# An adaLN, H3 and SwiGLU kernel on one core: the front of the program in another order, with both half loads of modulation rows ahead of the third chunk's return

## The chip, the core and the metric

The kernel runs on one core of a Trainium2 chip. The metric is the device time of one execution in microseconds, and every figure below is for that one core. A difference of 0.2% is about 1.2 us here.

## What is computed

The sequence has S = 2048 positions and D = 512 channels, the feed-forward layer F = 1792 columns. Everything is float32.

```python
mod = (silu(c) @ w_mod).reshape(1, 6, 1, 512)      # six modulation rows
sa, ca, ga, sb, cb, gb = mod[:, 0], ..., mod[:, 5]
h = layernorm(x) * (1 + ca) + sa
# H3 mixer with q = h
k_shift = causal_conv4(k, shift_k)                 # four taps for each channel
kv = k_shift * v
y = irfft(rfft(kv, 2 * S) * rfft(ssm_k, 2 * S))[:S] + kv * ssm_D
x = x + ga * (h * y)
h = layernorm(x) * (1 + cb) + sb
x = x + gb * ((silu(h @ w_gate) * (h @ w_up)) @ w_down)
```

## The kernel before

The channels are worked in four chunks of 128. For each chunk c the program builds `kv` on VectorE (`tap`, `times_v`), turns it and takes the first stage of its Fourier transform on TensorE (`x_turn`, `x_first`), does the same for the long filter (`k_first`, `k_turn`), and swaps 32x32 blocks on VectorE (`swap_x`). The second stage, the product with the filter and the first inverse stage go by halves of a chunk, numbered n = 2c and 2c + 1: `x3` and `x_sum` make three inputs, `product3` multiplies them with three filter products, `inv3` goes back. For chunks 0, 1 and 2 the result X must be turned through memory: `put(c)` writes 2 MB to DRAM, and `get(c)` fetches it back with rows and positions exchanged, in four DMAs of 512 KB. For chunk 3 that turn is done by VectorE straight out of PSUM (`inv3s`). "The third chunk's return" in the title is `get(2)`.

`y_pe(t, *cs)` takes the last inverse stage for position tile t (512 positions) and chunks cs; it needs the matrix `ei` (`load_einv`) and the returned chunks. VectorE gates the result and adds it to x (`y_gate` with `add_y`, or `y_into` in one, which also collects the statistics of the second layernorm). The first layernorm's gate is made ahead of that by `gate_n` (ScalarE) and `gate_p` (GpSimd or VectorE). The modulation rows come in three parts `wm` of 2 MB, loaded in halves; for the third part `mod_row(2, h)` does a half's products on TensorE, `mod_out` copies the row out, `mod_T` turns it into columns.

The second layernorm of tile t ends in `rs1` (VectorE), `rs2` and `rs3` (GpSimd), four `norm1` (ScalarE). Then four `norm_t` transpose on TensorE, `norm_s` scales, and `hi1` and `lo1` split each operand into a high part and a low rest. `gu_pe` is the first gate and up product of the feed-forward layer. `warm(n)` issues n matmuls whose result nobody reads. The feed-forward loop that follows (seven products in place of eight, weights split and kept) is the longest part of the kernel.

What stands where is written out by hand: between the lines 1204 and 1595 some 390 calls stand in a list, and every engine works through its own instructions in the order of that list, since each helper issues with `keep_in_program_order`. All loads and stores are issued by SyncE on one queue, in the order of the list as well. Eight DMA semaphores go round, so a DMA is issued only when the one eight places before it has landed. Buffers come from tagged pools, and the strings in `SLOTS` say which buffer each new tile takes; `ps` gives the four pairs of PSUM banks. A tile that takes a buffer waits for the last reader of the tile before it. The third part of the modulation rows shares its buffer with the first-stage filter of chunk 3, so its load waits for the last `k_turn(3, ...)`:

```python
def mod_load(p_, h=None):
    if p_ not in WM:
        WM[p_] = (f16 if p_ == 2 else b16)("wm", (P, 8, D))
    for k in (0, 1) if h is None else (h,):
        t = slice(4 * k, 4 * k + 4)
        sp.dma_start(WM[p_][:, t], wmod[p_][:, t])
```

Every instruction is recorded at line 40, the helper that keeps the order, so the profile is read by the names of the tiles: `iv` is `inv3`, `pk` is `product3`, `px` is `x3`, `kt` is `k_turn`, `s` on TensorE a first stage, `y` is `y_pe`, `mr` is `mod_row`, `pm` is `mod_T`, `nt` is `norm_t`, `g` is `gu_pe`, `away` the DRAM copy of a chunk, `wm` a part of the modulation rows, `ei` the matrix of the last inverse stage, `ss` the long filter, `rsb` the second layernorm's scale. A `dn` is a down product; `a`, `b` and `c` are products of the feed-forward loop.

Of the kernel before, what the change touches and what calls it, by code (L numbers as in the profile page):

```python
# [43 lines left out]
def adaln_h3_swiglu(ctx, tc, q, k0, v0, kT, vT, ssm, dskip, wgu, wdn, wmod, e_fwd, e_inv, w_c, out):  # L44
# [9 lines left out]
        "e8": "301245670142561074612740340143104134104134104134150364051304650314056304",  # L54
        "b16": "0112345024024453024",
        "k2": "012021021020121020121020121020121020121020121012021012021012021012021012021012021012",
        "ps": "012301230123012031203120312031203120312013201320132013210321032103103210321032103210321032102310231023102310321032103210321213120023012120310",
        "r4": "01234012430012342013424301430123403402143201342014320134201432013420143240310234213014324031",
        "one": "456723017425036241736412506425173421750621507341573062570634170346250362417364125064251730256731546317027513643105725601341076526370140753623157047561321065745630120376546713025",
# [299 lines left out]
    def swap_x(n):  # L359
        swap(X[n // 4], n % 4)  # L360
# [842 lines left out]

    load_k0(0)
    diag(0, e=act)
    diag(2, e=dve)
    load_k0(1)
    warm(16)
    small_in(e=act)
    p_tap0(e=dve)  # L1210
    p_tap(1, 0, e=dve)
    p_tap(2, 0, e=dve)
    load_v0(0)
    load_k(1)
# [24 lines left out]
    load_ssm(0, 1)
    load_ssm(0, 2)  # L1240
    load_ssm(0, 3)
    load_v(1)
    room()
    tap(1, 1)
    tap(1, 2)
    skip(0, e=dve)
    load_k(2)
    tap(1, 3)
    times_v(1, 3, e=pool)
    load_v(2)  # L1250
    swap_x(2)
    swap_x(3)
    k_first(0, 2, e=act)
    k_first(0, 1, e=act)
    times_v(1, 2, e=pool)
    k_first(0, 3, e=act)
    times_v(1, 1, e=pool)
    k_first(0, 0, e=act)
    tap0(2, e=act)
    warm(5)  # L1260
    k_turn(0, 0, e=act)
    k_turn(0, 1, e=dve)
    tap(2, 1)
    times_v(1, 0, e=pool)
    k_turn(0, 2, e=act)
    x_turn(1, 1, e=act)
    k_turn(0, 3, e=act)
    tap(2, 2)
    load_ssm(1)
    x_turn(1, 0, e=act)  # L1270
    k_first(1, 3, e=act)
    skip(1, e=pool)
    k_first(1, 0, e=act)
    x_first(1, 0, e=act)
    k_first(1, 1, e=act)
    k_first(1, 2, e=act)
    mod_rep(e=dve)
    x_first(1, 1, e=act)
    load_wc()
    load_k(3)  # L1280
    k_turn(1, 0, e=act)
    k_turn(1, 3, e=act)
    tap(2, 3)
    times_v(2, 0, e=pool)
    times_v(2, 1, e=pool)
    tap0(3, e=dve)
# [12 lines left out]
    tms(3, 2, e=act)
    tap(3, 1)  # L1300
    x_sum(0, e=pool)
    tma(3, 2, 3, e=pool)
    swap_x(4)
    x_turn(2, 1, e=act)
    tma(3, 2, 1, e=pool)
    tma(3, 2, 2, e=pool)
    swap_x(6)
    tms(3, 3, e=act)
    tma(3, 3, 3, e=pool)
    product3(1, 1)  # L1310
    tma(3, 3, 1, e=pool)
    mod_load(0)
    tma(3, 2, 0, e=pool)
    tma(3, 3, 0, e=pool)
    product3(0, 0)
    load_ssm(3)
    mod_mul(0, 0, e=act)
    load_ssm(2)
    product3(1, 2)
    product3(0, 1)  # L1320
    product3(0, 2)
    product3(1, 0)
    k_turn(1, 2, e=act)
    x_first(2, 1, e=act)
    swap_x(7)
    swap_x(5)
    load_v(3)
    mod_load(1)
    swap_x(8)
    mod_part(0, 0, e=pool)  # L1330
    load_x(0)
    tma(3, 3, 2, e=pool)
    load_einv()
    times_v(3, 1, e=pool)
    skip(2, e=dve)
    mod_mul(0, 1, e=act)
    times_v(3, 2, e=pool)
    inv3(1, e=act)
    inv3(0, e=act)
    put(0)  # L1340
    load_x(2)
    load_x(3)
    times_v(3, 3, e=pool)
    k_turn(1, 1, e=act)
    swap_x(10)
    x3(3, 2, e=dve)
    x3(2, 1, e=act)
    x3(3, 1, e=act)
    swap_x(9)
    skip(3, e=dve)  # L1350
    times_v(3, 0, e=pool)
    k_first(2, 0, e=act)
    k_first(2, 2, e=act)
    x_sum(3, e=dve)
    get(0)
    x3(2, 2, e=act)
    x_sum(2, e=pool)
    mod_mul(1, 0, e=act)
    mod_part(1, 0, e=pool)
    product3(3, 2)  # L1360
    product3(3, 0)
    product3(3, 1)
    mod_mul(1, 1, e=act)
    product3(2, 0)
    product3(2, 2)
    mod_part(1, 1, e=pool)
    mod_part(0, 1, e=pool)
    mod_part(0, 2, e=pool)
    do_stats(1, 0)
    mod_part(1, 2, e=pool)  # L1370
    product3(2, 1)
    k_first(2, 3, e=act)
    k_first(2, 1, e=act)
    x_turn(3, 0, e=act)
    inv3(3, e=act)
    inv3(2, e=act)
    do_stats(2, 0)
    k_turn(2, 0, e=act)
    x_turn(3, 1, e=act)
    k_turn(2, 1, e=act)  # L1380
    k_turn(2, 3, e=act)
    swap_x(11)
    put(1)
    get(1)
    x_first(3, 0, e=act)
    mod_part(0, 3, e=pool)
    mod_part(1, 3, e=pool)
    mod_bc(1)
    do_stats(0, 0)
    do_stats(0, 1)  # L1390
    do_stats(1, 1)
    x_first(3, 1, e=act)
    do_stats(2, 1)
    mod_bc(0)
    x3(5, 1, e=act)
    x3(5, 2, e=act)
    x3(4, 2, e=act)
    k_turn(2, 2, e=act)
    do_stats(3, 0)
    do_stats(3, 1)  # L1400
    x3(4, 1, e=act)
    x_sum(4, e=pool)
    swap_x(14)
    x_sum(5, e=pool)
    mod_mix()
    gate_n(2, 0, e=dve)
    k_first(3, 1, e=act)
    k_first(3, 0, e=act)
    k_first(3, 2, e=act)
    gate_n(0, 0, e=act)  # L1410
    gate_p(0, 0, 1, e=pool)
    load_w(1)
    k_first(3, 3, e=act)
    gate_n(3, 0, e=act)
    swap_x(15)
    swap_x(12)
    gate_n(0, 1, e=act)
    gate_p(0, 2, 1, e=pool)
    gate_n(1, 0, e=act)
    product3(4, 0)  # L1420
    product3(4, 2)
    gate_n(2, 1, e=act)
    product3(5, 0)
    product3(4, 1)
    product3(5, 1)
    product3(5, 2)
    swap_x(13)
    inv3(4, e=act)
    inv3(5, e=act)
    k_turn(3, 0, e=act)  # L1430
    k_turn(3, 2, e=act)
    gate_p(0, 3, 1, e=pool)
    put(2)
    k_turn(3, 1, e=act)
    gate_p(2, 0, 1, e=dve)
    gate_p(2, 2, 1, e=dve)
    x3(7, 1, e=act)
    x3(7, 2, e=act)
    gate_p(1, 0, 1, e=dve)
    mod_load(2, 0)  # L1440
    get(2)
    mod_load(2, 1)
    x_sum(7, e=pool)
    y_pe(0, 0, 1)
    gate_n(3, 1, e=act)
    gate_p(3, 0, 1, e=dve)
    gate_p(3, 2, 1, e=pool)
    k_turn(3, 3, e=act)
    gate_p(0, 1, 1, e=dve)
    x3(6, 1, e=act)  # L1450
    y_into(0, 0, 1)
    x3(6, 2, e=act)
    x_sum(6, e=pool)
    product3(7, 0)
    product3(7, 2)
    product3(7, 1)
    product3(6, 0)
    gate_n(1, 1, e=act)
    gate_p(1, 3, 1, e=pool)
    w8_hi(1)  # L1460
    product3(6, 1)
    gate_p(1, 1, 1, e=pool)
    product3(6, 2)
    inv3s(7)
    inv3s(6)
    y_pe(2, 0, 1)
    gate_p(2, 1, 1, e=pool)
    gate_p(2, 3, 1, e=pool)
    y_gate(2, 0, 1)
    y_pe(1, 0, 1)  # L1470
    gate_p(1, 2, 1, e=pool)
    mod_row(2, 0)
    load_w(0)
    y_pe(0, 3)
    gate_p(3, 1, 1, e=pool)
    y_into(0, 3)
    y_pe(0, 2)
    mod_row(2, 1)
    mod_out(2, e=act)
    w8_lo(1, e=pool)  # L1480
    y_into(0, 2)
    y_pe(2, 2, 3)
    rs1(0)
    mod_T()
    y_pe(1, 2, 3)
    rs2(0)
    rs3(0)
    y_pe(3, 0, 1)
    w8_hi(0)
    w8_lo(0, e=pool)  # L1490
    norm1(0, 0, e=act)
    norm1(0, 1, e=act)
    load_w(2)
    load_wd(0)
    wd_mul(0, e=pool)
    norm1(0, 2, e=act)
    norm1(0, 3, e=act)
    norm_t(0, 0)
    norm_s(0, 0, e=act)
    hi1("B11", 0, e=act)  # L1500
    y_gate(2, 2, 3)
    warm(5)
    norm_t(0, 1)
    norm_s(0, 1, e=act)
    acts_room()
    wd_hi(0)
    y_into(1, 0, 1)
    y_into(1, 2, 3)
    rs1(1)
    norm_t(0, 2)  # L1510
    norm_t(0, 3)
    norm_s(0, 2, e=act)
    hi1("B11", 1, e=act)
    lo1("B11", 1, e=dve)
    norm_s(0, 3, e=act)
    lo1("B11", 0, e=pool)
    hi1("B21", 0, e=act)
    gate_p(3, 3, 1, e=pool)
    y_gate(3, 0, 1)
    add_y(3, 0, 4, (0, 1), e=dve)  # L1520
    rs2(1)
    rs3(1)
    y_pe(3, 2, 3)
    lo1("B21", 0, e=pool)
    y_gate(3, 2, 3)
    norm1(1, 0, e=act)
    norm1(1, 1, e=act)
    gu_pe(0, 0, 0)
    hi1("B21", 1, e=act)
    lo1("B21", 1, e=dve)  # L1530
    add_y(3, 0, 4, (2, 3), e=dve)
    norm1(1, 2, e=act)
    room()
    gu_pe(1, 0, 0)
    gu_pe(1, 0, 1)
    gu_pe(0, 0, 1)
    load_w(3)
    norm1(1, 3, e=act)
    gu_pe(0, 0, 2)
    norm_t(1, 0)  # L1540
    norm_t(1, 1)
    add_y(2, 0, 4, (2, 3), e=dve)
    norm_s(1, 0, e=act)
    hi1("B12", 0, e=act)
    norm_t(1, 2)
    norm_t(1, 3)
    norm_s(1, 1, e=dve)
# [231 lines left out]
```

## Time and profile before

| | us |
|---|---|
| median of 3 runs | 581.48 |
| lowest and highest | 580.92 and 582.07 |
| the profiled execution, its own time | 579.46 |
| its span in the profile | 577.7 |
| TensorE busy in the span | 571.7 (99%) |
| VectorE busy in the span | 448.3 (78%) |
| ScalarE busy in the span | 306.4 (53%) |
| GpSimd busy in the span | 318.0 (55%) |
| first product of the feed-forward loop (`a`) starts | 182.11 |

A time of the profile counts from the start of the span. An engine's share over the whole span is a mean of two unlike stretches: the front up to about 182 us, where all five engines have much to do, and the loop behind it, where TensorE alone is full. The queue of SyncE, called SPq, issues the DMAs, and the time from issue to landing is the DMA's.

### The profile page before, as it was taken

The numbers are of one execution on the slowest core, as the hardware profiler recorded it, in microseconds if no ns is written. First come the engines' busy times: TensorE is split into PE (matmuls) and PEld (weight loads), VectorE is DVE, ScalarE is ACT, GpSimd is POOL, SyncE is SP. The second block draws the span as 40 slices with busy tenths as digits, with TensorE's granted clock in tenths as the row PEclk, the third lists the DMA queues.
The fourth block names the chain that finished last, engine by engine and source line by source line (L and its number), as shares of the span: only waits on it lengthen the run. The fifth ranks groups of instructions, "written<-read, shape, count | busy, mean of one in ns | idle before, by whom it ended". The sixth has DMA issues, their size and how long they took to land.

```text
span 577.7 us, 10729 instructions
## 1 busy us (share of the span) xinstructions
PE 571.7 (99%) x4262; PEld 462.5 (80%) x4262; DVE 448.3 (78%) x622; ACT 306.4 (53%) x471; POOL 318.0 (55%) x298
## 2 busy tenths in 40 slices
PE   9999999999999999999999999999999999999997
PEld 9985476546888888888887888888888888888886
DVE  4999999998998766666576579858686868686766
ACT  3999989951754544445454566343424343434330
POOL 1349897689737866757475676461606161515210
PEclk9999999999999999999999999999999999999999
DMA  8966998998215454284939970454343434343403
GB/s 315 411 256 261 379 251 227 235 235 205 69 37 200 148 216 165 40 281 145 283 140 257 250 319 1 149 190 171 117 160 124 160 123 161 127 162 127 163 1 145
DMA packets 54435, 106.98 MB, mean 185 GB/s; under 512 B 19441, under 2 KB 36209, under 8 KB 48370
## 3 DMA queue, kind: packets, MB, share of 16 engines
q1 hardware_dynamic: 54386, 106.31, 56.0%
q8 instruction: 33, 0.54, 0.4%
q14 instruction: 16, 0.13, 0.1%
HBM read 71.69 MB, written 34.60 MB: 184 GB/s over the span
## 4 chain that ended last, share of the span: by engine, by line
PE 86%; DVE 5%; DMA 4%; ACT 1%; SPq 1%; issue 1%; POOL 0%; ACTq 0%; POOLq 0%; DVEq 0%
PE a L40 22%; PE dn L40 14%; PE c L40 11%; PE b L40 6%; PE da L40 6%; PE s L40 4%; PE g L40 4%; PE dc L40 3%; PE iv L40 3%; PE pk L40 3%; DMA wm<-in_wmod 2%; PE kvt L40 2%; PE px L40 2%; DMA away<-X 1%; PE kt L40 1%; PE db L40 1%
## 5 line engine op out<-in xcount | busy, mean ns | idle before, releaser
L40 PE MATMUL a<-op,wsum 128*128 128x512 f32 x432 | 110.9, 392 | 0.3 <-ACT r L40 0.2
L40 PEld LDWEIGHTS a<-op,wsum 128*128 128x128 f32 x432 | 78.7, 188 | 15.7 <-ACT r L40 0.7
L40 PE MATMUL dn<-wd,acts 128*128 128x512 f32 x360 | 90.4, 389 | 0.0
L40 PEld LDWEIGHTS dn<-wd,acts 128*128 128x128 f32 x360 | 67.5, 188 | 14.0
L40 ACT COPY p<-a 128x512 f32<-128x512 f32 x50 | 29.3, 587 | 57.2 <-PE a L40 57.2
L40 POOL TENSOR_TENSOR wa<-ws,wa 128x512 fp32r<-128x512 f32 (+1 forms) x28 | 32.9, 1196 | 41.1 <-ACT wa L40 41.1
L40 DVE TENSOR_TENSOR x<-x,dn 128x512 f32<-128x512 f32 (+1 forms) x65 | 43.4, 672 | 12.8 <-PE dn L40 12.5
L40 POOL TENSOR_TENSOR tb<-wds 128x256 f32<-128x256 f32 x12 | 8.9, 740 | 64.1 <-DVE wds L40 64.1
L40 DVE TENSOR_TENSOR b<-r,c 128x512 f32<-128x512 f32 x24 | 16.7, 696 | 32.9 <-ACT sg L40 32.9
L40 ACT COPY r<-a 128x512 f32<-128x512 f32 x24 | 14.1, 586 | 50.7 <-PE a L40 50.7
L40 PE MATMUL c<-op,wa 128*128 128x512 f32 x156 | 40.0, 392 | 0.0
L40 PE MATMUL c<-op,wsum 128*128 128x512 f32 x156 | 39.6, 389 | 0.0
L40 DVE STREAM_TRANSPOSE X<-X 128x1024 f32<-128x1024 f32 x16 | 37.6, 2415 | 0.8 <-ACT X L40 0.8
L40 POOL TENSOR_TENSOR wsum<-sr,wsum 128x512 fp32r<-128x512 f32 x28 | 38.1, 1381 | 0.0
L40 PE MATMUL b<-op,wa 128*128 128x512 f32 x144 | 36.9, 391 | 0.0
L40 POOL TENSOR_TENSOR wd<-wds,wd 128x512 fp32r<-128x512 f32 x14 | 18.3, 1329 | 29.1 <-ACT wd L40 29.1
L40 PEld LDWEIGHTS c<-op,wsum 128*128 128x128 f32 x156 | 29.3, 188 | 6.1
L40 DVE TENSOR_TENSOR x<-x,da 128x512 f32<-128x512 f32 x48 | 32.7, 681 | 1.2 <-PE da L40 1.1
L40 PEld LDWEIGHTS c<-op,wa 128*128 128x128 f32 x156 | 28.5, 188 | 5.7 <-DVE b L40 0.4
L40 PEld LDWEIGHTS b<-op,wa 128*128 128x128 f32 x144 | 26.3, 188 | 4.9
L40 POOL TENSOR_TENSOR s<-s,bcs 128x512 f32<-128x512 f32 x22 | 28.0, 1287 | 0.9
L40 POOL TENSOR_TENSOR sr<-ws 128x256 f32<-128x256 f32 x28 | 24.8, 885 | 5.3 <-issue 4.4
(193 smaller groups left out, 1351.1 us busy)
## 6 DMA issues: line engine op xcount, KB each, us to landing
ds<-wsum SPq DMA_DIRECT2D x12, 1024.0 KB, 8.0
wsum<-ds SPq DMA_DIRECT2D x12, 1024.0 KB, 6.4
dw<-wa SPq DMA_DIRECT2D x12, 768.0 KB, 6.3
wa<-dw SPq DMA_DIRECT2D x12, 768.0 KB, 4.3
ws<-in_wgu SPq DMA_DIRECT2D x16, 512.0 KB, 5.4
wds<-in_wdn SPq DMA_DIRECT2D x14, 512.0 KB, 7.1
wm<-in_wmod SPq DMA_DIRECT2D x6, 1024.0 KB, 10.1
away<-X SPq DMA_DIRECT2D x3, 2048.0 KB, 11.8
```

The costliest lines, as they stand in the source:

```text
L40: return lambda *a, **k: self.tc.keep_in_program_order(f(*a, **k))
```

## The change

Only the list of calls and the `SLOTS` strings differ; every helper and the loop behind the front are the same text. Nearly every line of the list has another place. The sum of the work hardly changes: the same 26 `warm` matmuls in other places, the four `skip` instructions on one row of `ss` on GpSimd where three were on VectorE, and some elementwise steps on other engines. The places that the prediction speaks of, cut from the diff, with one of the `SLOTS` strings:

```diff
-        "b16": "0112345024024453024",
+        "b16": "0123450202530015430",
...
+    warm(5)
     load_k0(0)
...
+    skip(3, e=pool)
+    x_sum(3, e=pool)
...
-    warm(5)
...
-    load_einv()
...
-    skip(3, e=dve)
...
-    x_sum(3, e=dve)
...
+    load_einv()
...
+    warm(5)
...
+    put(2)
...
+    mod_load(2, 0)
+    mod_load(2, 1)
...
-    put(2)
...
-    mod_load(2, 0)
-    get(2)
-    mod_load(2, 1)
...
+    get(2)
...
+    mod_row(2, 0)
+    mod_row(2, 1)
+    y_pe(2, 0, 1)
...
+    mod_T()
...
     y_pe(0, 3)
...
     y_pe(0, 2)
-    mod_row(2, 1)
...
+    rs2(0)
...
-    mod_T()
...
-    warm(5)
...
+    add_y(2, 0, 4, (0, 1), e=pool)
```

On SyncE's queue the place is the return of the third chunk, with a `put` and a `get` of a chunk ahead of it (the numbers at the names tell tiles apart, and differ between the two programs). Before:

```order
L40 DMA away_1108<-X_400 128x4096
L40 DMA X_400<-away_1108 32x32x128 x4
L40 DMA ws<-in_wgu 128x1024
L40 DMA away_1498<-X_558 128x4096
L40 DMA wm<-in_wmod 128x2048
L40 DMA X_558<-away_1498 32x32x128 x4
L40 DMA wm<-in_wmod 128x2048
L40 DMA ws<-in_wgu 128x1024 x2
```

And in the change:

```order
L40 DMA away_1292<-X_413 128x4096
L40 DMA X_413<-away_1292 32x32x128 x4
L40 DMA ws<-in_wgu 128x1024
L40 DMA ei<-in_e_inv 128x2048
L40 DMA away_1482<-X_753 128x4096
L40 DMA wm<-in_wmod 128x2048 x2
L40 DMA X_753<-away_1482 32x32x128 x4
L40 DMA ws<-in_wgu 128x1024
```

The second half of the modulation rows has moved from behind the four DMAs of the return to ahead of them, and the load of `ei`, which stood far ahead of this place, now stands behind a load of weights (`ws`).

On TensorE the place is what follows the last inverse stage of chunk 3. Before, with X_195, X_400, X_558 and X_1114 for chunks 0 to 3:

```order
L40 MATMUL iv<-xs,wc 64x512 x48
L40 MATMUL y<-X_195,ei 64x128 x8
L40 MATMUL y<-X_400,ei 64x128 x8
L40 MATMUL y<-X_195,ei 64x128 x8
L40 MATMUL y<-X_400,ei 64x128 x8
L40 MATMUL mr<-wm,crep 32x512 x8
L40 MATMUL y<-X_1114,ei 64x128 x8
L40 MATMUL y<-X_558,ei 64x128 x8
L40 MATMUL mr<-wm,crep 32x512 x8
L40 MATMUL y<-X_558,ei 64x128 x8
L40 MATMUL y<-X_1114,ei 64x128 x8
L40 MATMUL pm<-thirty,mrow 128x1 x8
```

In the change, with X_203, X_413, X_753 and X_1118 for the same chunks:

```order
L40 MATMUL iv<-xs,wc 64x512 x48
L40 MATMUL mr<-wm,crep 32x512 x16
L40 MATMUL y<-X_203,ei 64x128 x8
L40 MATMUL y<-X_413,ei 64x128 x8
L40 MATMUL pm<-thirty,mrow 128x1 x8
L40 MATMUL y<-X_1118,ei 64x128 x8
L40 MATMUL y<-X_753,ei 64x128 x16
L40 MATMUL y<-X_1118,ei 64x128 x8
L40 MATMUL y<-X_753,ei 64x128 x8
L40 MATMUL y<-X_1118,ei 64x128 x8
L40 MATMUL y<-X_203,ei 64x128 x8
L40 MATMUL y<-X_413,ei 64x128 x8
```

Both halves of the modulation row and its turn `pm` now stand ahead of the first `y` that reads chunk 3 or chunk 2, and one pair of `y` that stood there has gone behind.

On GpSimd the place is the end of the second layernorm of tile 0 and what follows it. Before:

```order
L40 TENSOR_TENSOR s_1290<-s_1290,bcs 128x512 x2
L40 TENSOR_TENSOR wg<-ws,wg 128x512 x2
L40 TENSOR_TENSOR rsb_1864<-rsb_1864,mhalf 128x4
L40 TENSOR_TENSOR rsb_1864<-rsb_1864 128x4
L40 TENSOR_TENSOR wg<-ws,wg 128x512 x2
L40 TENSOR_TENSOR wds<-wds,bcs 128x1024
L40 TENSOR_TENSOR op<-hraw,op 128x512
L40 TENSOR_TENSOR s_1290<-s_1290,bcs 128x512 x2
```

In the change:

```order
L40 TENSOR_TENSOR s_1353<-s_1353,bcs 128x512 x2
L40 TENSOR_TENSOR rsb_1849<-rsb_1849,mhalf 128x4
L40 TENSOR_TENSOR rsb_1849<-rsb_1849 128x4
L40 TENSOR_TENSOR wg<-ws,wg 128x512 x2
L40 TENSOR_TENSOR wds<-wds,bcs 128x1024
L40 TENSOR_TENSOR op<-hraw,op 128x512
L40 TENSOR_TENSOR x_718<-x_718,s_1368 128x4x256
L40 TENSOR_TENSOR op<-hraw,op 128x512
```

An addition into x (`add_y`) now stands on GpSimd between the low rests of two operands of the first feed-forward product.

More of the change, by code (lines that the diff above doesn't have):

```diff
@@ L1314, in adaln_h3_swiglu @@
[L1314 to L1319, printed above, removed]
+    x3(0, 2, e=act)
+    tms(3, 2, e=dve)
+    x3(0, 1, e=act)
+    x_sum(0, e=pool)
+    times_v(2, 3, e=pool)
+    skip(2, e=pool)
+    product3(1, 0)
+    tms(3, 3, e=act)
+    mod_mul(1, 1, e=act)
+    mod_load(0)
+    product3(1, 1)
+    product3(1, 2)
+    times_v(2, 1, e=pool)
+    k_turn(1, 0, e=dve)
+    mod_mul(1, 0, e=act)
     product3(0, 1)
     product3(0, 2)
-    product3(1, 0)
@@ new lines, in adaln_h3_swiglu @@
+    x_first(2, 0, e=act)
+    x_first(2, 1, e=act)
+    swap_x(5)
+    k_first(2, 0, e=act)
+    k_first(2, 3, e=act)
+    x3(2, 1, e=act)
+    swap_x(7)
+    x3(2, 2, e=act)
+    x3(3, 1, e=act)
+    x3(3, 2, e=act)
+    k_first(2, 2, e=act)
+    do_stats(2, 0)
+    swap_x(10)
+    swap_x(11)
+    x_sum(2, e=pool)
+    product3(2, 1)
+    product3(2, 2)
+    mod_mul(0, 0, e=act)
+    k_first(2, 1, e=act)
+    mod_rep(e=act)
+    product3(2, 0)
+    skip(3, e=pool)
+    x_sum(3, e=pool)
+    mod_mul(0, 1, e=act)
@@ L1368, in adaln_h3_swiglu @@
+    product3(3, 2)
+    product3(3, 1)
+    product3(3, 0)
+    times_v(3, 1, e=pool)
+    inv3(2, e=act)
+    inv3(3, e=act)
+    x3(5, 1, e=act)
+    times_v(3, 0, e=pool)
+    x_turn(3, 0, e=act)
+    k_turn(2, 0, e=act)
+    k_turn(2, 2, e=act)
+    times_v(3, 3, e=pool)
+    times_v(3, 2, e=pool)
+    mod_part(0, 1, e=pool)
+    mod_part(0, 0, e=pool)
+    x_turn(3, 1, e=act)
+    k_turn(2, 3, e=act)
+    k_turn(2, 1, e=act)
+    load_x(3)
+    room()
     mod_part(0, 2, e=pool)
+    load_x(1)
@@ L1369, in adaln_h3_swiglu @@
+    mod_part(0, 3, e=pool)
+    x_first(3, 0, e=act)
     do_stats(1, 0)
[L1370 to L1386, printed above, removed]
+    x_first(3, 1, e=act)
+    mod_bc(0)
     mod_part(1, 3, e=pool)
-    mod_bc(1)
@@ new lines, in adaln_h3_swiglu @@
+    get(0)
+    k_first(3, 1, e=act)
+    swap_x(15)
+    put(1)
+    k_first(3, 0, e=act)
+    k_first(3, 3, e=act)
+    k_first(3, 2, e=act)
+    product3(5, 2)
+    mod_bc(1)
+    mod_mix()
+    product3(4, 0)
+    gate_n(1, 0, e=act)
+    gate_p(1, 0, 1, e=pool)
+    product3(4, 1)
+    gate_n(2, 0, e=act)
+    gate_n(0, 0, e=act)
+    get(1)
+    product3(5, 1)
+    product3(4, 2)
+    gate_n(3, 0, e=act)
+    gate_n(3, 1, e=act)
+    load_w(2)
+    load_einv()
+    gate_p(0, 0, 1, e=pool)
@@ L1519, in adaln_h3_swiglu @@
-    y_gate(3, 0, 1)
-    add_y(3, 0, 4, (0, 1), e=dve)
+    hi1("B21", 0, e=act)
+    room()
+    norm_s(0, 3, e=act)
+    add_y(2, 0, 4, (0, 1), e=pool)
+    y_pe(3, 0, 1)
+    gu_pe(1, 0, 0)
+    y_gate(3, 0, 1)
+    gu_pe(0, 0, 0)
+    norm_s(0, 1, e=act)
+    hi1("B11", 1, e=act)
+    lo1("B11", 1, e=pool)
+    gu_pe(0, 0, 1)
+    gu_pe(1, 0, 1)
     rs2(1)
     rs3(1)
-    y_pe(3, 2, 3)
-    lo1("B21", 0, e=pool)
-    y_gate(3, 2, 3)
     norm1(1, 0, e=act)
-    norm1(1, 1, e=act)
-    gu_pe(0, 0, 0)
@@ L1529, in adaln_h3_swiglu @@
-    hi1("B21", 1, e=act)
-    lo1("B21", 1, e=dve)
-    add_y(3, 0, 4, (2, 3), e=dve)
-    norm1(1, 2, e=act)
[L1533 to L1537, printed above, removed]
-    norm1(1, 3, e=act)
[L1539 to L1544, printed above, removed]
+    hi1("B21", 1, e=dve)
+    lo1("B21", 0, e=dve)
+    gu_pe(0, 0, 2)
+    norm1(1, 1, e=dve)
+    norm1(1, 2, e=act)
+    norm1(1, 3, e=act)
```

417 lines of the change are left out of this document (182 added, 235 removed).

## The prediction

> **What bounds the kernel now.** I read the page's busy times first, to see which engine can set the span, then the busy times by stage for the front, then the chain of waits around the third chunk's return, and last the rows of TensorE where a group took longer than its like. The page and the table by stage:
>
> ```profile
> PE 571.7 (99%) x4262; PEld 462.5 (80%) x4262; DVE 448.3 (78%) x622; ACT 306.4 (53%) x471; POOL 318.0 (55%) x298
> ...
> 100.00:125.00 25.00, 25.00 (x416) 12.93 (x400) 23.96 (x31) 23.28 (x30) 18.15 (x15) 1.00 1.02 246
> 125.00:150.00 25.00, 24.26 (x371) 17.08 (x356) 22.84 (x41) 6.29 (x8) 23.12 (x19) 1.00 0.77 173
> ```
>
> TensorE is busy for 571.7 of 577.7 us, so a new order of the same instructions can win only what TensorE loses to waits. In the two stages, columns PE, PEld, DVE, ACT, POOL, TensorE is full too, but VectorE has 24.0 and 22.8 of 25 us, GpSimd 23.1 in the second: hardly any engine has room, and a wait moved to another engine soon comes back to TensorE. The chain of waits through the return, with its end:
>
> ```profile
> 112.17 8.44 DMA away<-X
> ...
> 126.40 12.98 DMA wm<-in_wmod
> 139.39 0.04 issue
> 139.43 1.09 PE mr L40 x16
> 140.53 1.90 PE y L40 x32
> 142.42 1.88 PE pm L40 x16
> 144.30 3.65 PE y L40 x64
> 147.94 0.59 PE nt L40 x4
> 148.53 1.12 PE warm L40 x10
> 149.65 1.31 PE nt L40 x12
> 150.96 1.96 PE y L40 x32
> 152.92 7.03 PE g L40 x30
> ...
> 182.11 1.36 PE a L40 x6
> ```
>
> The store of chunk 2 must land before its return is issued; the second half of the modulation rows is issued behind that, takes 12.98 us and lets `mr` begin at 139.43. From there on the chain is TensorE's own, to the first product `a` of the loop at 182.11, behind which nothing of the order changes. So the forecast is how far that start moves. Rows of TensorE that took longer than the same group elsewhere:
>
> ```profile
> 22.25 1.38 PE L40 MATMUL warm<-ident 128*128 128x128 f32 x10
> 23.85 0.60 PE L40 MATMUL kt<-ident,kt 128*128 128x128 f32 x3 [0.22 <-ACT kt L40]
> ...
> 55.59 5.41 PE L40 MATMUL iv<-xs,wc 32*64 32x512 f32 x96
> ...
> 104.76 6.00 PE L40 MATMUL iv<-xs,wc 32*64 32x512 f32 x96
> ...
> 125.48 6.65 PE L40 MATMUL iv<-xs,wc 32*64 32x512 f32 x96
> 132.06 3.71 PE L40 MATMUL y<-X,ei 128*64 128x128 f32 x64
> 135.71 1.09 PE L40 MATMUL mr<-wm,crep 64*32 64x512 f32 x16
> 136.73 1.97 PE L40 MATMUL y<-X,ei 128*64 128x128 f32 x32
> 139.43 1.09 PE L40 MATMUL mr<-wm,crep 64*32 64x512 f32 x16 [0.74 <-DMA wm<-in_wmod]
> ```
>
> The five warm calls at 22.25 hold TensorE for 1.60 us up to the next group. The `iv` at 104.76 takes 0.6 us more than the one at 55.59 (6.00 against 5.41), the last one at 125.48 takes 1.2 more, and the wait for the modulation rows costs 0.74. Together that is some 3 us, the most that this change can take back in the front.
>
> **The change, part by part.** I carry one landmark: the `y` at 136.73, the first that reads chunk 3. Ahead of it TensorE now does more: the second half of `mr` (1.09), `pm` (1.88), five more warm calls at the start (1.12 by the row at 148.53) and five ahead of the `iv` that stood at 104.76 (1.12); it does less by the warm calls at 22.25 (1.60) and by one pair of `y` (1.90). The sum is +1.71.
>
> The waits on the way. The four `skip` now all stand on GpSimd:
>
> ```profile
> L40 POOL TENSOR_TENSOR ss<-ss,bcs 1x128 f32<-1x128 f32 x1 | 2.7, 2665 | 1.3 <-DMA ss<-in_ssm 1.3
> ...
> L40 DVE TENSOR_TENSOR ss<-ss,bcs 1x128 f32<-1x128 f32 x3 | 0.9, 294 | 0.0
> ```
>
> One takes 2.67 us there and 0.29 on VectorE. For chunks 0 and 2 other work lies between it and its reader; `skip(1)` was on GpSimd already. `skip(3)` is now followed there by `x_sum(3)`, and the `product3` of that half, which overwrites what `x_sum` reads, waits for both. That delays TensorE by between 0 (VectorE is late as well) and 2.4 us (2.67 less 0.29, nothing to hide it); I take 0.7, nearer to the lower end, since three products of the other half, which are not concerned, stand in front. Against it stands the 0.6 of the `iv` at 104.76, which now has five warm calls before it while VectorE finishes the products. The `iv` at 125.48 keeps its 1.2: VectorE, which feeds it, has no less ahead of it. Waits net +0.1, so the landmark moves to 136.73 + 1.71 + 0.1 = 138.5.
>
> What then stands behind the landmark is the end of the second layernorm of tile 0. Its rows, by engine:
>
> ```profile
> 137.87 0.70 DVE L40 TENSOR_TENSOR y<-y,s 128x512 f32<-128x512 f32 x1 [0.81 <-PE y L40]
> ...
> 140.11 0.68 DVE L40 TENSOR_TENSOR y<-y,s 128x512 f32<-128x512 f32 x1
> ...
> 143.24 1.02 POOL L40 TENSOR_TENSOR rsb<-rsb,mhalf 128x4 f32<-128x4 f32 x1 [0.68 <-DVE rsb L40]
> ...
> 144.57 2.94 ACT L40 ACTIVATE n<-x,rsb 128x512 f32<-128x512 f32 x4 [1.94 <-POOL rsb L40]
> 148.57 0.78 ACT L40 ACTIVATE hraw<-nt,modT 128x512 f32<-128x512 f32 x1 [1.06 <-PE nt L40]
> 149.38 0.62 ACT L40 CAST op<-hraw 128x512 fp32r<-128x512 f32 x1
> ```
>
> VectorE begins 1.14 us after the `y` does, and from there to the last `norm1` at 147.51 (144.57 + 2.94) it is 9.64 us through VectorE, GpSimd and ScalarE. Before, TensorE came to `nt` at 147.94, 0.4 us later, and did not wait. Now: 138.5 + 1.14 + 9.64 = 149.3 for the last `norm1`, while TensorE has from the landmark only the two halves of a pair (1.90) and four pairs of `y` (7.60) and is there at 148.0. So 1.3 us of **new wait at `norm_t`**, in place of the 0.74 for `mr`. From 149.3: four `nt` (0.59 + 1.31) and a pair of `y` (1.96) give 153.2. The first `g` takes banks that ScalarE's fifth step behind `nt` sets free: 149.3 + 0.63 (148.57 less 147.94) + about 3.6 (three steps of 0.78 and two of 0.62) = 153.5. Before, `g` began at 152.92, and the same TensorE work follows: +0.6. Last, `lo1` of the operand's other half stands on GpSimd behind `add_y`:
>
> ```profile
> 146.97 2.38 POOL L40 TENSOR_TENSOR wds<-wds,bcs 128x1024 f32<-128x1024 f32 x1
> ```
>
> That addition, priced by this row of its size at 2.4 to 2.6 us, stands behind the first operand's `lo1`; by the steps above it ends about 155.2 and the next `lo1` at 156.5, where TensorE is at 156.35: another 0.15. The end moves by +0.75 us.
>
> **The return.** The rows of SyncE's DMAs and of the traffic (last column GB/s):
>
> ```profile
> DMA to landing us min/median/max: 12.5/13.0/13.5
> ...
> 123.59 2.77 SPq L40
> ...
> 120.60:126.40 5.80, 5.80 (x107) 1.76 (x91) 5.80 (x12) 3.37 (x5) 5.64 (x6) 1.00 1.10 275
> 126.40:137.10 10.70, 10.70 (x178) 6.13 (x176) 10.66 (x7) 0.00 (x0) 10.39 (x9) 1.00 1.18 228
> 137.10:139.40 2.30, 1.59 (x30) 1.35 (x26) 1.46 (x3) 0.00 (x0) 2.22 (x3) 1.00 1.00 399
> ```
>
> The last of the four return DMAs was issued at 123.59 and landed 13.5 later, at 137.1, 16.5 after the store had landed (120.61). TensorE now gets to the store's last producer about 1.1 us later, so the store lands at 121.75. Lower bound: the return is no slower for one more MB ahead of it, 138.2. Upper bound: that MB goes wholly ahead at the 399 GB/s of the last row, 2.6 us: 140.8. I take 139.5, the middle. TensorE comes to `y` on chunk 2 at 139.45, but VectorE starts on it only 2.24 us after the first (140.11 less 137.87), at 141.9; so a landing up to 140.7 (1.2 us ahead, for the `y` and the step to VectorE) costs nothing that the wait at `norm_t` doesn't hold already.
>
> [...] The trace does not bear out a strict order: the half issued behind the return took 12.98 us, and only 2.3 us of that lie behind the return's landing.
>
> **The sum**: the profiled execution took 579.46, of which 577.7 is span; with +0.75 it would be 580.2. The median of the runs shown, 581.48, lies 2.0 above it, and I put the change on the median: 582.2.
>
> **Rivals.**
>
> *Faster, the waits just go.* If GpSimd's steps hide and the third `iv` loses its 1.2, the landmark comes at 138.5 − 0.7 − 1.2 = 136.6, and the return becomes the bound: at its lower end, 138.2, VectorE can start on chunk 2 at 139.4, and the rest of the layernorm (9.64 − 2.24) ends at 146.8, 2.5 before the forecast's 149.3; at the middle, 139.5, 1.2 before it. The end moves by −0.5 to −1.8; 580.2 for −1.3. For it: the long `iv` and the wait for `wm` stand in rows that the change touches. Against: VectorE's 24.0 of 25 us. Chance 0.22.
>
> *Slower, the return comes late.* If both halves, the return and the weight loads behind it (1 MB more) share the queue at the 228 GB/s of the row, some 4.6 MB after 121.75 take 20.2 us: landing at 141.9, 1.2 beyond the deciding 140.7, and a us for each further us, since `norm_t`, four `nt` and all of `g` stand behind it. The end moves by +1.95, 583.4; with the store also a us late, 584.4. For it: 2 MB stand ahead instead of 1. Against: 399 GB/s in the last row. Chance 0.23.
>
> *Slower, the helpers fall behind.* GpSimd has 23.1 of 25 us before and gets `skip` and `add_y` in addition. With the full 2.4 for `skip(3)` in place of 0.7, the end moves by +2.45: 583.9. The load of `ei`, now behind a weight load that waits for an `iv`, could add to that. Chance 0.15.
>
> *It changes nothing* because TensorE's work is the same: that lies inside the forecast's band, with which it shares 0.40.
>
> **The numbers.** 0.2%, about 1.2 us, is what a measurement of this kernel can tell from no change; it spans 580.3 to 582.6. Forecast and no effect together 0.40, both in it: same 0.40. Faster 0.22; the slower rivals 0.23 + 0.15 = 0.38. The range reaches from 579.6 (just beyond the faster rival's −1.8) to 585.1 (both slower rivals at once, 0.75 + 1.2 + 1.7 = +3.65). The likeliest case by itself spans 581.3 to 582.6.
>
> **What would show it.** Right: no wait for `wm` at `mr`; `nt` of tile 0 waits for ScalarE by about 1.3 us; the return lands between 138.2 and 140.8; `a` starts near 182.9; GpSimd's `ss` rows take 2.7 each. Wrong: TensorE waits for `X<-away` by over a us, or for `ei`; `nt` doesn't wait; `a` starts before 181 or after 184.

## The result, and the profile after

The changed kernel took 586.87 us (median of 4 runs, 585.03 to 587.23) against 581.20 (4 runs, 580.37 to 582.07) for the kernel before: 1.0090 times the time, 95% interval 1.0071 to 1.0109. It is slower by 5.7 us, beyond the range of 579.6 to 585.1.

The profiled execution took 585.03 us with a span of 583.2, against 579.46 and 577.7. The page's busy times, and the busy times by stage of the changed kernel (us, then PE, PEld, DVE, ACT, POOL, the granted clock, DMA share, GB/s):

```profile
span 583.2 us, 10718 instructions
PE 573.1 (98%) x4262; PEld 465.1 (80%) x4262; DVE 449.8 (77%) x623; ACT 305.8 (52%) x473; POOL 309.4 (53%) x295
...
100.00:125.00 25.00, 22.67 (x334) 12.29 (x338) 24.62 (x32) 21.59 (x27) 15.43 (x13) 1.00 0.79 214
125.00:150.00 25.00, 23.44 (x370) 15.96 (x356) 22.50 (x35) 5.40 (x7) 22.42 (x19) 0.93 0.88 199
```

TensorE has as many instructions as before and only 1.4 us more of busy time, yet it now idles 2.3 us in the first of these stages and 1.6 in the second, where before it idled 0 and 0.7. The second stage also has a granted clock of 0.93 in place of 1.00. The chain of waits through the return:

```profile
116.44 8.42 DMA away<-X
...
126.84 4.73 SPq L40
...
131.61 11.82 DMA X<-away
143.43 0.25 issue
143.68 9.52 PE y L40 x144
153.20 0.60 PE nt L40 x4
...
157.31 7.14 PE g L40 x30
...
186.64 1.36 PE a L40 x6
```

The loop's first product starts at 186.64, 4.53 later than before (182.11). Another 1.0 of the 5.5 us of span lies in the loop, mostly in one wait of 0.9 at a `c`, which I have not followed further; in the variants below the loop is some 0.3 to 2.2 longer than before. The store of chunk 2 leaves at 116.44 in place of 112.17, and the return has landed at 143.43 in place of 137.1, which is 18.6 us after its store (landed at 124.86) in place of 16.5. SyncE's queue was held up as well: the issue of the return's third piece took 4.73 us where it took 1.95 before, so that the fourth could be issued only at 131.61. TensorE's waits in the front, and its rows at the two places:

```profile
PE pk L40 <- DVE xs L40: 2.3, 2, 1.9
PE y L40 <- DMA X<-away: 1.6, 1, 1.6
```

```profile
100.40 1.95 PE L40 MATMUL pk<-K,wc 64*32 64x512 f32 x32
104.26 1.95 PE L40 MATMUL pk<-K,wc 64*32 64x512 f32 x32 [1.91 <-DVE xs L40]
106.59 1.09 PE L40 MATMUL pk<-K,wc 64*32 64x512 f32 x16 [0.38 <-DVE xs L40]
...
139.15 1.95 PE L40 MATMUL pm<-thirty,mrow 128*128 128x1 f32 x16
141.02 1.09 PE L40 MATMUL y<-X,ei 128*64 128x128 f32 x16
143.68 9.52 PE L40 MATMUL y<-X,ei 128*64 128x128 f32 x144 [1.56 <-DMA X<-away]
```

The products `pk` of chunk 2 wait for VectorE's `xs`, the multiplications that take earlier products out of their banks, and the `y` on chunk 2 waits for the return. Why VectorE is late shows in its own rows 20 us earlier:

```profile
80.60 0.69 DVE L40 BATCH_NORM_STATS2 bna<-x 128x6 f32<-128x512 f32 x1 [3.14 <-DMA x<-in_q]
```

It stood 3.14 us for the load of x tile 1. In the order before, tile 1 was loaded first of the four and its statistics stood first; in the change it is loaded last (issued at 71.7, landed at 80.6) and its statistics still stand ahead of those of tiles 3 and 0, with most of what VectorE has to do for chunk 2 behind them. Last, the granted clock (third column from the end) at the wait for the return:

```profile
141.00:146.00 5.00, 3.44 (x39) 3.21 (x41) 2.80 (x9) 0.00 (x0) 4.84 (x5) 0.73 0.68 200
146.00:150.00 4.00, 4.00 (x72) 4.00 (x70) 3.90 (x14) 1.05 (x1) 1.97 (x3) 0.92 0.00 0
```

By slices of 0.25 us the granted clock is 0.50 from 143.25 to 146.67, for 3.4 us. It fell 1.1 us into the wait, which runs from 142.12 to 143.68, and not at its end. TensorE works in 3.0 of the 3.4 us, so at 0.50 it loses some 1.5 by estimate; measured, the 144 `y` of that row take 9.52 us, where they take 8.08 in the two variants below that wait there and kept the clock, and TensorE's busy time has grown by 1.4. The three losses, 2.3 at `pk`, 1.6 at the return and 1.5 of clock, less the 0.74 for `wm` that is gone, make some 4.6 us, and so account for the 4.53.

### The profile page after: what moved, and what is told of

It is laid out like the page before. It is cut to its first block, busy times and chain, and to the rows that moved or that the text cites. A ratio compares the mean times of both kernels' runs of the same rounds, so it can differ in the third digit from the quotient of the medians.

```text
span 583.2 us, 10718 instructions
## 1 busy us (share of the span) xinstructions
PE 573.1 (98%) x4262; PEld 465.1 (80%) x4262; DVE 449.8 (77%) x623; ACT 305.8 (52%) x473; POOL 309.4 (53%) x295
## 4 chain that ended last, share of the span: by engine, by line
PE 81%; ACT 6%; DMA 6%; DVE 3%; issue 2%; SPq 1%; POOL 0%; ACTq 0%; POOLq 0%
PE a L40 21%; PE dn L40 12%; PE c L40 11%; PE da L40 6%; PE b L40 6%; PE g L40 4%; PE dc L40 3%; PE iv L40 3%; PE s L40 3%; PE kvt L40 2%; PE pk L40 2%; DMA X<-away 2%; PE kt L40 2%; PE y L40 2%; PE px L40 2%
## 5 line engine op out<-in xcount | busy, mean ns | idle before, releaser
L40 POOL TENSOR_TENSOR xs<-xs 128x512 f32<-128x512 f32 x14 | 17.7, 1287 | 23.9 <-ACT xs L40 23.9
```

What stands on the lines that cost most here:

```text
L40: return lambda *a, **k: self.tc.keep_in_program_order(f(*a, **k))
```

## The experiments

The theory after the comparison: three separate costs, **A** the statistics of x tile 1 that stand in front of a late load, **B** a return that lands later because both half loads stand ahead of it, **C** a clock that halves at the wait. The rivals: the whole delay is one early one that is carried on, with the queue's order harmless; or VectorE is simply too full, and A comes back wherever the statistics are put. All ratios below are to the kernel before, run beside the variants on the same chip. The diffs leave out the `ps` string of `SLOTS`, which is set to suit wherever a call that takes banks has moved.

**A taken away: the statistics of tiles 0 and 1 exchanged.**

```diff
-    do_stats(1, 0)
+    do_stats(0, 0)
...
-    do_stats(1, 1)
+    do_stats(0, 1)
...
-    do_stats(0, 0)
+    do_stats(1, 0)
...
-    do_stats(0, 1)
+    do_stats(1, 1)
```

> The changed kernel with tiles 0 and 1 exchanged in the first layernorm's statistics, so that VectorE no longer stands at tile 1, whose load has not landed. Theory (the 3.1 us for which VectorE waits for that load push the block swaps and the products of chunk 2 back): the wait at 77.5 goes, the pk group at 100.4 falls from 7.3 to 4.4 to 5 us, and the end moves by -2.5 to -3 us, to about 584 us. Rival (ScalarE's full stretch from 85 to 100 us sets those products): VectorE waits elsewhere, pk stays above 6.5 us, less than 1 us is won. On the return: if it is late because two halves stand ahead of it, TensorE still waits 1 to 2 us for X<-away; if it was late only because its store was, that wait goes too and the time is near 581.5 us.

Measured: 582.65 us (10 runs), 1.0025 [1.0006, 1.0044]. TensorE's waits in the front:

```profile
PE y L40 <- DMA ei<-in_e_inv: 1.3, 1, 1.3
PE y L40 <- DMA X<-away: 1.2, 1, 1.2
```

The wait at `pk` is gone, and 3 to 4 us with it: A is a misplaced pair of calls, not a lack of room on VectorE. The front now comes early enough to show what stood hidden behind A, the load of `ei` behind the weight load, and the return is still late: it landed at 141.83, 19.6 us after its first piece was issued (122.20), where that is 16.5 before and 18.6 in the change. Six of the ten runs have a clock of 0.997 or less; the profiled one, with waits of 1.3 and 1.2, has the full clock.

**B alone, put into the kernel before.**

```diff
     mod_load(2, 0)
-    get(2)
     mod_load(2, 1)
+    get(2)
```

> The kernel before with one edit: the second half load of modulation rows is issued ahead of the third chunk's return. Theory (two halves ahead make the return late): the return lands 18 to 19 us after its store instead of 16.5, about 139, TensorE waits about 1.3 us for it at the y of chunk 2 in place of 0.74 for wm; +0.5 us, or +1 to +2 us (583) if the granted clock falls behind that wait. Rival (the halves are no burden, the store was late): the return lands at 137 to 138, the wait for wm goes, 580.5 to 581.2 us.

Measured: 583.05 us (10 runs), 1.0036 [1.0013, 1.0059]. Waits and clock:

```profile
PE y L40 <- DVE bnb L40: 2.9, 1, 2.9
...
141.00:146.00 5.00, 5.00 (x56) 2.99 (x52) 3.03 (x12) 2.19 (x3) 2.79 (x5) 0.66 0.41 116
```

The return landed at 139.96, 18.8 us after its store instead of 16.5: one more MB ahead of it cost 2.3 us. The wait of 2.9 is put down to `bnb`, but that had ended at 139.65 and the `y` began at 140.16, right after the landing; in the kernel before the same `y` runs 2 us ahead of the end of that `bnb` and does not need it. So B is worth 2 us by itself, with nothing else of the new order there. Part of that is again the clock: the six runs at 0.999 or more have a median of 582.0, 0.9 above the kernel before, the four at 0.997 or less one of 584.3.

**C: the wait filled with work.** Seven `warm` calls in front of the `y` on chunk 2 in the change:

```diff
     y_into(0, 3)
+    warm(7)
     y_pe(0, 2)
```

> The changed kernel with seven warm calls (1.6 us of matmuls that nobody reads) put where TensorE waits for the third chunk's return. Theory (the wait itself costs 1.7 us and the halved clock behind it another 1.4): the matmuls fill the wait, the granted clock stays 1.00 between 141 and 150 us, the y run at full rate at once, and the end moves by -0.8 to -1.4 us, to about 585.7 us. Rival (the slow y are not a matter of the clock, or the clock falls anyway): no change, or +1.6 us if the matmuls stand in the way, 586.9 to 588.5 us.

Measured: 583.97 us (10 runs), 1.0052 [1.0031, 1.0074]; six of the ten have a clock of 0.999 or more. In the profiled execution:

```profile
PE pk L40 <- DVE xs L40: 1.5, 2, 1.1
...
PE y L40 <- DMA X<-away: 0.7, 1, 0.7
...
141.00:146.00 5.00, 4.30 (x62) 3.97 (x60) 3.26 (x8) 0.30 (x1) 4.84 (x5) 1.00 0.60 172
```

The filling did no useful work, the return came no earlier (143.59), and the kernel still gained some 2 us over the change, more than the 0.8 to 1.4 expected, though the two intervals overlap. Ten of eleven runs of the change have a clock of 0.997 or less, and here four of ten: the clock was a cost of its own.

**The wait filled with another `y`** (that of tile 1 on chunks 0 and 1, from behind it):

```diff
     y_into(0, 3)
+    y_pe(1, 0, 1)
     y_pe(0, 2)
...
-    y_pe(1, 0, 1)
     y_into(1, 0, 1)
```

> The changed kernel with the y of tile 1, chunks 0 and 1 (1.9 us of useful work that needs no return) moved ahead of the first y that reads chunk 2, with the banks exchanged to suit. Theory: it fills the wait, the y of chunk 2 start at 143.8 at full rate; VectorE's, GpSimd's and ScalarE's steps of the second layernorm then end about 0.7 us earlier, and TensorE waits about 1.9 us for them at norm_t; the end moves by -0.7 us (586.2) if the clock holds there, and by 0 to +0.5 us if it falls there instead. Rival (only TensorE's idle time counts): -1.7 to -3 us, 584 to 585 us.

Measured: 585.08 us (6 runs), 1.0067 [1.0046, 1.0087], where 586.2 or more was expected; three of the six runs have a clock of 0.997.

```profile
PE nt L40 <- ACT n L40: 1.5, 3, 0.8
```

The wait for the return has gone, and 1.5 us of waiting comes back at `norm_t`, from 150.0 on: what is needed is chunk 2, and useful work in front of it mostly moves the wait. That is the place at which the prediction expected 1.3.

**`ei` ahead of the weight load**, on top of the exchanged statistics:

```diff
-    load_w(2)
     load_einv()
+    load_w(2)
```

> The first experiment's kernel (statistics of tiles 0 and 1 exchanged) with the load of ei ahead of the weight load it stood behind. Theory (in that kernel TensorE waits 1.3 us for ei because the load is issued only when an iv has run): the wait for ei goes, the store of chunk 2 lands about as before, TensorE comes 1.3 us earlier to the return, whose landing depends on the store and on the two halves, so most of it turns into a longer wait for X<-away (2 to 2.5 us), and the clock falls in more executions: 0 to -1 us against that kernel's 582.65, 581.7 to 583. Rival (the waits add up): -1.3 us or more, 581.3 or less, with the wait for X<-away unchanged at 1.2 us.

Measured: 582.61 us (12 runs), 1.0026 [1.0010, 1.0042]; no gain over 582.65. The wait for `ei` is gone and the one for the return took its place:

```profile
PE y L40 <- DMA X<-away: 1.4, 1, 1.4
...
138.18 1.09 PE L40 MATMUL y<-X,ei 128*64 128x128 f32 x16
...
128.35 12.12 DMA X<-away
182.47 1.36 PE a L40 x6
```

Its runs sort by the mean granted clock of each run. The two with 0.999 or more took 580.43 and 580.93, five with 0.997 a median of 582.23, five with 0.994 one of 583.58. One stretch of 3.4 us at half the clock is 0.3% of the mean clock of a run; by these times a fall of 0.3% goes with some 1.5 us, and one of 0.6% with 2.9. So B and C are not separate here: the return still lands late in the profiled execution, at 140.47, but the two runs that kept the clock, it among them, are no slower than the kernel before. As far as two runs show it, what B costs in this order comes through the clock.

**B taken away as well: the return between the halves**, with the second half's products behind the `y` on chunk 2.

```diff
     mod_load(2, 0)
+    get(2)
     mod_load(2, 1)
...
-    get(2)
...
     mod_row(2, 0)
-    mod_row(2, 1)
     y_pe(2, 0, 1)
...
-    mod_out(2, e=act)
-    mod_T()
+    y_pe(1, 0, 1)
...
     y_pe(0, 2)
+    mod_row(2, 1)
+    mod_out(2, e=act)
...
     y_gate(3, 2, 3)
+    mod_T()
...
-    y_pe(1, 0, 1)
```

> The kernel of e5 with the return of the third chunk issued between the two half loads, as in the kernel before, and the second half's mr, its copy and pm moved behind the first y of chunk 2, the y of tile 1, chunks 0 and 1 ahead of it in their place; the banks are set to suit. Theory (descriptors of the one queue go in order, so each half ahead of the return delays it by 2 to 2.6 us): the return lands 16 to 17 us after its store instead of 19 to 20, TensorE waits for it under 0.5 us, no clock falls behind it, and the layernorm of tile 0 is covered by y, mr and pm: 579.5 to 580.5 us, under the kernel before. Rival (the rest of the front's order is what costs): 582 or more, with new waits at y or nt.

Measured: 581.03 us (12 runs), 0.9999 [0.9988, 1.0010], with no run under a clock of 0.999. The return landed at 137.97, 16.2 us after its store. The gain expected over the kernel before did not come: TensorE is now early at the second half row and waits for it, as before. The edit also moves `pm` from just ahead of the wait for the return to a place behind it, so the landing shows B taken away, while the clock can have kept for either reason.

```profile
PE mr L40 <- DMA wm<-in_wmod: 1.0, 1, 1.0
...
PE g L40 <- DVE x L40: 0.3, 1, 0.3
```

**B taken away alone**: the last edit in the change, with statistics and `ei` as the change has them.

> The change with the return between the two half loads, the second mod_row and its mod_out and mod_T behind the y of chunk 2, and the y pair of tile 1 in their place; the statistics and the load of ei stand as in the change. If the loss has two independent parts, an early one (VectorE's wait for x tile 1, about 3 us in the profiled execution) and a late one (the return's wait and the halved clock behind it, about 3 us), then the late one goes and the early one stays: the pk wait of 1.5 to 2.3 us is there, no X<-away wait over 0.3, granted clock 1.00, time 583 to 584. If the later landing is only a consequence of the late front (the store is later by 4 us), nothing is won by the place in the queue: 585 to 587 as for the change.

Measured: 584.47 us (12 runs), 1.0047 [1.0029, 1.0065]. TensorE's row at `pk` and the stages of the profiled execution:

```profile
104.87 4.51 PE L40 MATMUL pk<-K,wc 64*32 64x512 f32 x48 [2.41 <-DVE xs L40]
...
106.00:107.00 1.00, 1.00 (x16) 0.27 (x8) 1.00 (x2) 1.00 (x2) 1.00 (x1) 0.50 1.25 177
...
141.00:146.00 5.00, 3.90 (x66) 2.59 (x64) 4.75 (x10) 0.00 (x0) 4.84 (x5) 1.00 0.89 345
```

In the profile the late part went and the early one stayed, so the two are separate; the time fell by 1.3 us against the change run beside it (585.76), with intervals that overlap. I had expected a clock of 1.00 and 583 to 584, and was wrong: behind the wait at `pk`, 2.4 us here, the clock is halved too (105.3 to 108.7), and 7 of the 12 runs have a clock of 0.997 or less.

**C alone, with A and `ei` mended**: seven `warm` calls in front of the `y` on chunk 2.

> The change with the order of the statistics swapped and ei ahead of the weight load (582.61 in 12 runs, 10 of them at a granted clock of 0.997 or 0.994), and seven warm matmuls ahead of the y on chunk 2, in the time TensorE waits for the return. If it is the halved clock behind that wait that costs the last part, no run shows less than 0.998 and the time is 580.7 to 581.3, though the landing is no earlier. If the cost is the wait itself, the time stays at 582.6 (the warm matmuls replace idle time only).

Measured: 581.05 us (12 runs), 1.0002 [0.9987, 1.0016], against 582.61 without the warm calls. Runs with a lower clock fell from 10 of 12 to 4 of 12, not to none; the eight others took 580.14 to 582.06, with a median of 580.4, although the return is as late. The profiled execution is one of the four:

```profile
136.85 1.95 PE L40 MATMUL pm<-thirty,mrow 128*128 128x1 f32 x16
138.72 1.09 PE L40 MATMUL y<-X,ei 128*64 128x128 f32 x16
139.75 3.04 PE L40 MATMUL warm<-ident 128*128 128x128 f32 x14
142.72 5.51 PE L40 MATMUL y<-X,ei 128*64 128x128 f32 x90
```

The clock halves at 140.1 with no idle TensorE just ahead of it. What stands ahead of it is `pm`, sixteen products with a single column each, which ended 1.3 us before.

**The second half row further behind**, in the version with all three mended:

```diff
     y_pe(0, 2)
-    mod_row(2, 1)
-    mod_out(2, e=act)
...
     y_pe(3, 2, 3)
+    mod_row(2, 1)
+    mod_out(2, e=act)
     y_gate(3, 2, 3)
-    mod_T()
...
     y_gate(2, 2, 3)
+    mod_T()
```

> The version with the return between the halves, statistics swapped and ei early (581.03), with the second mod_row and its mod_out behind the y on chunk 3 of tile 3 and mod_T behind y_gate(2,2,3). If TensorE's last waits there (1.0 for wm, 0.3 at g) go by that, 579.7 to 580.4, faster than the kernel before. If they come back as a wait of hi1 and g for the modulation columns, 581 or more.

Measured: 580.01 us (12 runs), 0.9982 [0.9969, 0.9995]: the fastest of all here, ahead of the kernel before by 1.0 us, with an interval that only just leaves out no change. No run is under 0.999.

```profile
140.03 1.97 PE L40 MATMUL y<-X,ei 128*64 128x128 f32 x32 [0.66 <-DVE x L40]
141.92 1.09 PE L40 MATMUL mr<-wm,crep 64*32 64x512 f32 x16
142.94 1.97 PE L40 MATMUL y<-X,ei 128*64 128x128 f32 x32
144.84 1.95 PE L40 MATMUL pm<-thirty,mrow 128*128 128x1 f32 x16
```

The `mr` that waited 0.74 before and 1.0 in the version above now finds its half there.

**The change once more**, for its time and clocks beside these:

> The change itself once more, for its time and its granted clocks beside the others on the same chip: 585 to 587, with clocks of 0.997 or 0.994 in most runs, if the halving behind the return's wait belongs to this order; all runs near 1.00 if it was chance in the profiled one.

Measured: 585.76 us (7 runs, 582.81 to 590.70), 1.0092 [1.0057, 1.0128]. Six of the seven runs have a clock of 0.994 or less, the first four runs of the change had 0.997 or 0.994; the kernel before has 0.999 or more in all of 103 runs beside the variants. The lower clock belongs to this order.

```profile
PE y L40 <- DMA X<-away: 2.0, 1, 2.0
PE pk L40 <- DVE xs L40: 1.6, 2, 1.2
...
141.50:141.75 0.25, 0.00 (x0) 0.00 (x0) 0.25 (x1) 0.00 (x0) 0.25 (x1) 1.00 1.02 285
...
142.00:142.25 0.25, 0.00 (x0) 0.00 (x0) 0.25 (x1) 0.00 (x0) 0.20 (x1) 0.50 1.08 387
...
141.00:146.00 5.00, 2.95 (x31) 2.86 (x29) 3.04 (x8) 0.09 (x1) 4.73 (x4) 0.59 0.50 165
146.00:150.00 4.00, 4.00 (x52) 4.00 (x51) 3.46 (x12) 1.31 (x2) 1.61 (x3) 0.65 0.00 0
```

Here the half clock lasted from 141.9 to 148.8, 6.9 us. It began 0.8 us into the wait, which runs from 141.12 to 143.17.

**`pm` away from the wait**: the version with warm calls, `mod_T` behind the `y` on chunk 3 of tile 3, and more warm calls in its place.

```diff
     mod_out(2, e=act)
-    mod_T()
...
-    warm(7)
+    warm(24)
     y_pe(0, 2)
...
     y_gate(3, 2, 3)
+    mod_T()
```

> The version with seven warm matmuls ahead of the y on chunk 2 (581.05; granted clock 0.996 in 4 of 12 runs, and in the profiled one the half clock came at 140.1 with no idle TensorE ahead of it, 1.3 us behind the pm matmuls of 128x1), with mod_T and so pm moved behind the y on chunk 3 of tile 3 and 24 warm calls in place of seven, so that TensorE has 128x128 matmuls in place of pm until chunk 2 is there. If the pm matmuls count for the clock as next to no work, no run shows 0.997 or less, and the time is 580.2 to 581. If it is the wait for chunk 2 alone, about as many runs as before show 0.996.

Measured: 585.01 us (5 runs), 1.0057 [1.0039, 1.0076], all at 0.999 or 1.00. The time says nothing, since I had sized the warm calls wrongly: 24 of them are 48 products and took 5.62 us. With 13:

> The version with pm moved behind the y on chunk 3 of tile 3, with 13 warm calls in place of 24 (24 held TensorE for 5.62 us, to 142.98, 1.4 us past the landing of chunk 2; 13 take 3.0). If the pm matmuls count for the clock as next to no work, no run shows 0.997 or less; the time is then 580.2 to 581.3, and the 585.01 with 24 was the warm calls' own length. If the wait for chunk 2 (here some 0.7 us, behind warm matmuls) is enough, about a third of the runs show 0.996.

Measured: 583.65 us (10 runs), 1.0043 [1.0026, 1.0061], again all at 0.999 or 1.00.

```profile
137.01 3.17 PE L40 MATMUL warm<-ident 128*128 128x128 f32 x26
140.35 2.84 PE L40 MATMUL y<-X,ei 128*64 128x128 f32 x48 [0.17 <-issue]
143.12 1.95 PE L40 MATMUL pm<-thirty,mrow 128*128 128x1 f32 x16
...
313.24 1.67 PE L40 MATMUL a<-op,wsum 128*128 128x512 f32 x6 [1.72 <-ACT r L40]
```

On the clock, 0 of 15 runs (five and ten) fell against 4 of 12: this speaks for `pm` ahead of the wait having a part in the fall. It does not prove it, since the time also holds more dense products than the seven warm calls gave. On the time I was wrong: 580.2 to 581.3 expected. Of the 3 us too much the profile shows 1.4 as a longer wait for ScalarE in the loop (1.72, where the version with seven warm calls has 0.34); the rest I cannot place.

## Why the prediction was wrong, step by step

**The sum held no VectorE wait (failed).** "Waits net +0.1" was built from GpSimd's `skip(3)` at 0.7, out of a row of 2.67 us. In the changed kernel that step took 0.45:

```profile
70.14 0.45 POOL L40 TENSOR_TENSOR ss<-ss,bcs 1x128 f32<-1x128 f32 x1
```

The real wait was A. The two orders of `load_x` and `do_stats` had it in the open: which tile is loaded last, and which one's statistics stand first on an engine that I had called full. I asked what was moved onto engines, and not what each engine's next instruction waits for. The first `y` that reads chunk 3 came at 141.02, and not at 138.5; the 2.5 us are the 2.3 at `pk` and small change. The rival "the helpers fall behind" priced the same `skip(3)` at its full 2.4 and failed with it; the load of `ei`, which it named beside, cost TensorE 1.3 us once A was gone.

**The return's landing (failed, in size).** Against a landing at 138.2 to 140.8 stands 143.43; 3.1 us of that are the store (124.86, not 121.75). From store to landing I had 16.5 to 19.1 with 17.75 in the middle; it was 18.6 here, and with both halves ahead also 18.8 (B alone), 19.6 (statistics exchanged, from the first piece's issue) and 18.4 (`ei` early). So the upper bound was the value to take. My reading of the 12.98-us row was wrong: of the half issued behind the return only 2.3 us lay behind the return's landing, but at the 399 GB/s of that stretch 2.3 us carry 0.9 of its 1 MB, which is just what a strict order looks like, with each load wholly behind the one issued before it. The landings stand in the order of issue in both profiled executions: before, the return's four pieces at 126.8, 129.8, 134.1 and 137.1 and the half behind them at 139.4; in the change, the halves at 127.73 and 131.99 and the return's pieces from 134.97 on. How the queue works inside, no run shows.

**The rival "the return comes late" (right in kind, too small).** Its mechanism and its place are those of B, and the variant that does B alone in the kernel before measured +2.0 us, where the rival gave +1.95. That the two agree is luck: the rival had the landing 20.2 us after the store, where it was 18.8, and no loss of clock, which is about half of the 2.0. What it lacked in the changed kernel was A underneath, and C on top.

**The new wait at `norm_t` (not there).** 1.3 us were forecast; TensorE came to `nt` at 153.13 and ScalarE had ended at 153.09. The wait for the return and the slow `y` had taken its place. It shows (1.5) in the variant with the other `y`, where TensorE does not wait in front of it.

**The clock (failed: put at nothing).** I had read the granted clock of before, 1.00 in every stage, and took it to stay, without a reason. At a wait of 1.6 us it halved for 3.4 us and cost 1.5 us more. In the two profiled executions of the change it fell 1.1 and 0.8 us into a wait and stood at 0.50 for 3.4 and 6.9 us. That it belongs to the order shows in the runs: a clock of 0.997 or less in 10 of 11 of the change and in none of 103 of the kernel before. What makes it fall they do not show.

**What was right.** `mr` no longer waits for `wm`. The `iv` at 104.76 lost 0.5 (it took 5.51 us, at 109.04). Against the forecast, the `iv` at 125.48, which was to keep its 1.2, lost 0.6 as well (6.01, at 129.43). The `lo1` behind `add_y` is nowhere on the chain. The rest of the path held, too, where A and the fall of the clock are away: the version with exchanged statistics and early `ei` has the full clock in its profiled execution, and there the first `y` that reads chunk 3 came at 138.18 (forecast 138.5), the return at 140.47 (138.2 to 140.8), the last `norm1` ended at 149.26 (149.3), `g` began at 153.17 (153.5) and `a` at 182.47 (182.9). Only the wait at `nt` did not show, since TensorE came to it at 148.73 and not at 148.0. So the sum failed by the two terms that it did not have, VectorE's wait and the clock, far more than by those that it had.

The medians put it together: the change 585.76, less A (with `ei`) 582.61, less B 584.47, less both 581.03, where the kernel before has 581.1. With both mended the new order is neither better nor worse than the old one by these runs. These medians hold the clock's share of A and of B: with either left, the clock falls in more than half of the runs (7 of 12 with A, 10 of 12 with B).

## What to carry to other kernels

When an order is rearranged, follow each engine's queue to its first instruction that needs a load, and compare with the order of the loads: one step in front of a late load held back all that the engine does for others (here VectorE by 3.14 us, TensorE by 2.3). Count the bytes ahead of a gather on its DMA queue: here 1 MB more delayed it by 2.3 us. Look at the granted clock behind a TensorE wait: here one of 1.6 us was followed by a halved clock for 3.4 us, some 1.5 us more; where the wait could not go, seven `warm` calls, put into it, won 1.6 us.

## What the runs showed of the hardware

In the profiled executions the clock fell inside a wait of 1.6 and of 2.0 us that stood 1 us behind `pm` (1.1 and 0.8 us after the wait began), 0.4 and 1.1 us behind the end of waits of 2.4 and 2.9 us, and once with no wait at all, 1.3 us behind `pm`. Two profiled executions with waits of 1.2 and 1.4 us behind `pm` kept the full clock, and so did the one with 13 warm calls at its wait of 1.7 us in the loop, between products of 512 columns. Runs with a clock under 0.998, by version, with the waits of 0.6 us and more in the front of its profiled execution (less the 1.3 us for `ident` at the very start, which all have):

| version | waits of TensorE (us) | runs |
|---|---|---|
| before | 0.7, 2.9 us ahead of `pm` | 0 of 103 |
| before, with both halves ahead of the return | 2.9, 5.6 us ahead of `pm` | 4 of 10 |
| the change, both times | 1.6 and 2.0 behind `pm`, 1.9 and 1.2 at `pk` | 10 of 11 |
| the change with seven warm calls | 1.1 at `pk`, 0.7 behind the warm calls | 4 of 10 |
| the change with another `y` | 0.9 at `pk`, 0.8 at `nt` | 3 of 6 |
| statistics exchanged | 1.3 for `ei`, 1.2 behind `pm` | 6 of 10 |
| statistics and `ei` mended | 1.4 behind `pm` | 10 of 12 |
| the same with seven warm calls | none | 4 of 12 |
| the same with `pm` behind, 24 and 13 warm calls | 0.7 and 0.6, 7 us or more ahead of `pm` | 0 of 15 |
| return between the halves alone | 2.4 at `pk`, 1.0 for `wm` | 7 of 12 |
| all mended | 1.0, 2.9 us ahead of `pm` | 0 of 12 |
| all mended, row further behind | 0.7, 4.8 us ahead of `pm` | 0 of 12 |

The versions in which it never fell have no other wait over 1.1 us in the front, and none just behind `pm`. That is no rule: three others, with seven warm calls or another `y`, have none over 1.2 us in their profiles and none just behind `pm` either, and the clock fell in 4 of 10, 3 of 6 and 4 of 12 of their runs, in which the waits may have been others. Whether `pm` has a part in it stays open.
